# Delta-rule attention and two FFNs: rooms of their own for the fourth matrix's words, one inverse norm per unit of keys

## The chip, the cores and the metric

The kernel runs on one core of one Trainium2 chip. The metric is the device time of one launch in microseconds; the number to compare is the median of several runs. One further execution is profiled; its rows are what is read here. The engines are TensorE (PE, with its weight loads as PEld), VectorE (DVE), ScalarE (ACT), GpSimd (POOL) and SyncE (SP), whose queue issues every DMA of this kernel.

## The reference, cut to what matters

```python
def _attn_ref(q, k, v, beta):                 # (4, 8, 768, 48), float32
    k_n = k / (np.linalg.norm(k, axis=-1, keepdims=True) + 1e-06)
    state = zeros((B, H, D, D))
    for t in range(S):
        y[:, :, t] = q[:, :, t] @ state
        v_old = state^T @ k_n[:, :, t]
        state = state + beta_t * outer(k_n[:, :, t], v_t - v_old)
    return y

x = y.transpose(0, 2, 1, 3).reshape(B * S, H * D)          # 3072 tokens x 384
h = x @ moe_w_in;   x = maximum(0.01 * h, h) @ moe_w_out   # 384 -> 2048 -> 384
h = x @ moe2_w_in;  out = (h - tanh(h)) @ moe2_w_out
```

The four weight matrices arrive as float64; every key is divided by its norm.

## The kernel before, in words

The sequence is cut into steps of 64 positions and units of two steps: 6 units, 12 steps. In a step the delta rule becomes products of 64 x 64 blocks, with a triangular system of two 32 x 32 halves that `inverses` solves row by row, for a whole unit at once, mostly on GpSimd. Float32 accuracy comes from float16 pairs: each operand is split into a high and a low part, and a product is three float16 products.

Everything is one long program written out by Python generators. `Plan` estimates when each engine is free and each tile ready. `layer(n, i)` writes TensorE's FFN products for step n, layer i, in the order (0,0), (1,0), (0,1), (1,1), (2,0), and so on, and between them `Side.step` takes pieces of the attention and weight generators whose operands the plan holds ready: `keys`, `grams`, `inverses`, `merges`, `queries`, `products`, `states`, `outputs`, and `weights`. Keys named in `done` and waited for with `wait` order the generators among themselves. Each engine then runs its instructions in the order written. Generators take their place by a time and a delay, `d_...`, from the table START, or from STEADY once "w2" is in `done`. `weights` is also a filler: its VectorE operations may be put in front of a VectorE operation that the plan expects to wait.

`weights()` turns the four matrices from float64 into float16 pairs, in the order first layer in, first layer out, second in, second out. A matrix comes in 16 chunks of 128 x 768 int32 words, loaded by SP into "rooms": parts of weight tiles that are not in use yet. `w_f32` puts a chunk's words together as float32 in the destination tile (a `tensor_scalar` and two `scalar_tensor_tensor`); two chunks whose rooms lie side by side are taken as one, 768 wide, otherwise 384 wide each. ScalarE sums their squares into `wacc`, writing its by-product over the used room. When all are done, a norm across partitions gives the scale `sw`, and `splits` makes 16 pairs of parts: ScalarE twice (`wst<-wo`, `wo<-wst`), then VectorE or GpSimd once.

For the fourth matrix (`wo` number 1, second layer out) half of the chunks use rooms inside its own destination. The other eight use `Ub` and `Sb`, the operands with which `outputs` multiplies, so that the conversion waits for step 1's outputs and `outputs` from step 2 on waits for "w2". Layer (0,1) is the first that needs its splits.

`keys(n)` loads step n's keys, squares and sums them on ScalarE (16 pairs of instructions), computes 1 / (norm + 1e-6) in `key_scale` from a power of two as first guess and five Newton steps (22 VectorE operations on 128 x 16, tile `n`), and writes the scaled keys as float16 pairs (`kn`, `KN`). It starts once state n - 4 is done, as there are four `KN` tiles. The first two steps go through `first_keys`, both at once.

Of the kernel before, what the change touches and what calls it, by code (L numbers as in the profile page):

```python
# [7 lines left out]
F32 = mybir.dt.float32  # L8
F16 = mybir.dt.float16
BF16 = mybir.dt.bfloat16  # L10
I32 = mybir.dt.int32
ACTF = mybir.ActivationFunctionType
ALU = mybir.AluOpType
# [5 lines left out]
POW2 = 0x7F800000  # L19
# [172 lines left out]
def kernel(  # L192
# [12 lines left out]
    plan = Plan(tc.nc)  # L205
    pe, act, dve, pool, sp = (Engine(plan, n) for n in ("pe", "act", "dve", "pool", "sp"))
    NU, D = k.shape[0], k.shape[4]
    NM = k.shape[3]
# [32 lines left out]
    def tune(name):  # L241
        return (STEADY if "w2" in done else START)[name]
# [7 lines left out]
    def square_sum(o, i, junk):  # L250
        act.activation(out=junk if SIZE[junk.dtype] > 2 else junk.bitcast(BF16), in_=i, func=ACTF.Square, accum_out=o)
# [90 lines left out]
    def at(*aps):  # L342
        return plan.at(*aps)
# [6 lines left out]
    WO = [wts.tile([128, NF, 2, DM], F16, name=f"wo{i}") for i in range(2)]  # L350
    WI2 = [w.rearrange("p f c t n -> p f c (t n)") for w in WI]
    sw = const.tile([128, 6], F32, name="sw")

    def words(t):

        t = t.bitcast(I32)
        n = DM * 2
        return [t[:, i * n:(i + 1) * n] for i in range(t.shape[1] // n)]
# [64 lines left out]
    def weights():  # L423
        wi = [words(w.rearrange("p f c n -> p (f c n)")) for w in WI2]
        wo = [words(w.rearrange("p f c n -> p (f c n)")) for w in WO]
        nh = len(wi[0])

        x = [words(x_tile("w1"))[0] for _ in range(2)]
        a = Weights(0, w1_in, WI2[0], wo[0] + wo[1])
        b = Weights(1, w1_out, WO[0], ((wi[1] + x) * 2)[0:NF])  # L430
        yield Part([], 0)
        yield from a.convert()
        side.add(a.splits(), "s0")
        a = Weights(2, w2_in, WI2[1], (wo[1] * 2)[0:NF])
        yield from b.convert()
        side.add(b.splits(), "s1")
        done.add("w1")
        yield from a.convert()
        side.add(a.splits(), "s2")
        yield from wait(("y", 1))  # L440
        yield Part([], 0)
        bs = [words(t.rearrange("p c m n -> p (c m n)"))[0] for t in (Ub, Sb)]
        r = wo[1][nh // 2:] * 2 + bs * (NF // 4)
        b = Weights(3, w2_out, WO[1], r)
        yield from b.convert()
        for t in (Ub, Sb):
            pool.memset(t, 0.0)
        done.add("w2")
        side.add(b.splits(), "s3")

# [57 lines left out]
    def wait(key):  # L508
        if key not in done:
            yield lambda: key in done  # L510

    def load_k(n):
        if n < NS:
            kf_t[n] = ld_p.tile([128, NM, D], F32, tag="kf", name="kf", bufs=2)
            sp.dma_start(out=kf_t[n], in_=k[n // 2][:, n % 2])
# [35 lines left out]
    def key_scale(a, y, t):  # L551

        dve.tensor_scalar(out=t, in0=a, scalar1=2.0 ** -100, scalar2=None, op0=ALU.max)
        dve.tensor_scalar(out=y.bitcast(I32), in0=t.bitcast(I32), scalar1=1, scalar2=POW2,
                          op0=ALU.logical_shift_right, op1=ALU.bitwise_and)
        dve.tensor_scalar(out=t, in0=y, scalar1=2.0 ** 64 / 0.85, scalar2=None, op0=ALU.mult)
        dve.reciprocal(out=y, in_=t)
        for it in range(5):
            if it in (1, 3):
                yield plan.t["dve"]  # L560
            dve.tensor_tensor(out=t, in0=y, in1=y, op=ALU.mult)
            dve.scalar_tensor_tensor(out=t, in0=t, scalar=-0.5, in1=a, op0=ALU.mult, op1=ALU.mult)
            dve.scalar_tensor_tensor(out=y, in0=t, scalar=1.5, in1=y, op0=ALU.add, op1=ALU.mult)
        dve.tensor_tensor(out=t, in0=a, in1=y, op=ALU.mult)
        dve.tensor_scalar(out=t, in0=t, scalar1=1e-6, scalar2=1.0 / KS, op0=ALU.add, op1=ALU.mult)
        dve.reciprocal(out=y, in_=t)
# [8 lines left out]
            tt(kp[:, 1], kn, kp[:, 0], ALU.subtract, lead)  # L575
        done.add(("k", n))

    def keys(n):

        yield from wait(("s", n - 4))  # L580
        load_k(n)
        kf = kf_t.pop(n)
        n2 = sm_p.tile([128, 3, NM], F32, tag="n2", name="n2", bufs=1)
        a, y, t = (n2[:, i] for i in range(3))
        for m in range(NM):
            if m % tune("k_m") == 0:
                yield max(plan.t["act"], at(kf))
            junk = s_p.tile([128, D], BF16, tag="junk", name="junk", bufs=1)
            square_sum(a[:, m:m + 1], kf[:, m], junk)
        yield max(plan.t["dve"], at(a))  # L590
        yield from key_scale(a, y, t)
        yield max(plan.t["act"], at(y))
        key_split(n, kf, y, tune("lead_k"))

    def first_keys():

# [41 lines left out]
        split(AT[:, 0, av], AT[:, 1, av], ps[:, :, HB:], half[:, 0:1])  # L638

    def all_keys():  # L640
        for n in range(2, 2 * NU):
            yield from wait("w1")
            yield from keys(n)

    gd_t, nat_t = {}, {}

# [235 lines left out]
    def outputs(n):  # L882
# [3 lines left out]
        yield from wait(("x", u))  # L886
        Q, P = q_t.pop(n), p_t.pop(n)
        if n > 1:
            yield from wait("w2")
            yield from wait(("r", n - 3))  # L890
            yield from wait(x_owner[-NX])
            x_t[n] = x_tile(("a", n))
# [347 lines left out]
```

## Time and profile before

| | us |
|---|---|
| runs | 1243.42, 1246.35, 1244.53; median 1244.53 |
| profiled execution | 1241.99 |
| its span, first to last instruction | 1240.3 |
| TensorE busy in the span | 1012.0 |
| VectorE, ScalarE, GpSimd busy | 727.6, 635.0, 512.9 |
| mean granted TensorE clock | 0.959 |

Times in a row of the trace are microseconds from the start of the span. A row names the engine, the operation, what it writes and reads by the program's names, and how often. "idle before" is how long the engine did nothing ahead of it, and behind the arrow stands what ended that. All operations are recorded under line 160, where `Plan.issue` calls them, so rows are told apart by tiles. `h_ps` holds a first product of a layer, `o` a second, `a_ps` those of attention and norms.

### The profile page before, as it was taken

To read this page: it belongs to the slowest core of one execution; us is meant where nothing else is said; L and a number is where in the kernel's file an instruction comes from. 1 tells how busy PE (TensorE), PEld (TensorE's weight loads), DVE (VectorE), ACT (ScalarE), POOL (GpSimd) and SP (SyncE) were. 2 spreads that over 40 slices of the span, in tenths; PEclk is the share of its full clock that TensorE was granted. 3 is DMA by queue.
4 is the path that set the end of the run, shared out by engine and by line. 5 is a ranking of instruction groups with operands and counts; after the bars stand their busy time and mean duration, and the time that the engine had idled before them with its cause. 6 is when DMAs were issued, how large, how long until landed. Compare 5 with 4: busy or idle time off the path is not lost.

```text
span 1240.3 us, 36912 instructions
## 1 busy us (share of the span) xinstructions
PE 1012.0 (82%) x16216; PEld 832.3 (67%) x16216; DVE 727.6 (59%) x1609; ACT 635.0 (51%) x1414; POOL 512.9 (41%) x635
## 2 busy tenths in 40 slices
PE   0202679682876999989998899979999999999998
PEld 0202568571765788867687786768867888778875
DVE  7998844886768756776566577326654154420243
ACT  3556687746475555745455655325543354333342
POOL 4697365398238624771177304831210221012100
PEclk9999999895788999989999999989999999999999
DMA  9423010421000101000101000001000000000001
GB/s 359 160 72 112 3 28 18 164 60 39 16 25 23 45 16 46 23 23 3 27 15 37 12 24 10 14 14 32 25 10 14 14 11 2 1 17 11 1 1 26
DMA packets 21857, 48.17 MB, mean 39 GB/s; under 512 B 4288, under 2 KB 7360, under 8 KB 21696
## 3 DMA queue, kind: packets, MB, share of 16 engines
q1 hardware_dynamic: 21696, 45.82, 11.8%
q8 instruction: 126, 2.06, 0.7%
q14 instruction: 35, 0.29, 0.1%
HBM read 41.09 MB, written 4.72 MB: 37 GB/s over the span
## 4 chain that ended last, share of the span: by engine, by line
PE 54%; DVE 22%; ACT 13%; POOL 6%; issue 4%; DMA 1%; SPq 0%; ACTq 0%; POOLq 0%; DVEq 0%
PE o L160 22%; PE h_ps L160 21%; PE a_ps L160 10%; POOL X L160 2%; DVE n L160 2%; DVE wi L160 2%; DVE wo L160 2%; DVE x L160 2%; DVE sx L160 2%; ACT g L160 2%; POOL Gd L160 2%; ACT junk L160 2%; DVE g L160 2%; ACT sx L160 1%; DVE Ub L160 1%
## 5 line engine op out<-in xcount | busy, mean ns | idle before, releaser
L160 PE MATMUL h_ps<-x,wi 128*128 128x256 f16 x3456 | 422.5, 275 | 18.7 <-DVE x L160 6.3
L160 PEld LDWEIGHTS <-wi 128*128 128x128 f16 x3456 | 334.2, 98 | 76.5 <-issue 15.8
L160 PE MATMUL o<-wo,g 128*128 128x384 f16 x1152 | 213.2, 334 | 22.3 <-ACT wo L160 7.4
L160 POOL TENSOR_TENSOR g<-sx,g 128x512 f16<-128x512 f32 x80 | 96.2, 1203 | 314.5 <-ACT g L160 305.3
L160 PE MATMUL o<-g,wo 128*128 128x256 f16 x1728 | 211.0, 275 | 0.0
L160 PEld LDWEIGHTS <-wo 128*128 128x128 f16 x1728 | 167.2, 98 | 31.5 <-issue 9.3
L160 ACT ACTIVATE g<-sx 128x512 f16<-128x512 f32 x192 | 121.0, 630 | 119.5 <-DVE sx L160 116.5
L160 PEld LDWEIGHTS <-g 128*128 128x128 f16 x1152 | 112.5, 99 | 88.1 <-issue 27.1
L160 DVE SCALAR_TENSOR_TENSOR sx<-sx,kap,h_ps 128x512 f32<-128x512 f32 x96 | 71.2, 742 | 98.5 <-ACT sx L160 98.3
L160 POOL TENSOR_TENSOR X<-X,Gd 128x30 f32<-128x30 f32 (+9 forms) x180 | 116.1, 645 | 14.1
L160 POOL TENSOR_TENSOR Gd<-X 128x30 f32<-128x30 f32 (+9 forms) x180 | 108.4, 602 | 27.6 <-DVE X L160 15.2
L160 ACT ACTIVATE sx<-h_ps,kap 128x512 f32<-128x512 f32 x96 | 65.5, 683 | 92.2 <-PE h_ps L160 86.5
L160 ACT ACTIVATE sx<-h_ps 128x512 f32<-128x512 f32 x96 | 56.6, 590 | 105.5 <-PE h_ps L160 101.5
L160 DVE SCALAR_TENSOR_TENSOR g<-sx,g 128x512 f16<-128x512 f32 x96 | 71.4, 743 | 64.7 <-ACT g L160 64.6
L160 PEld LDWEIGHTS <-KTp 64*64 64x64 f16 x3360 | 66.4, 119 | 36.0 <-issue 34.5
L160 PE MATMUL a_ps<-ab,ones 128*128 128x1 bf16 x124 | 11.4, 168 | 95.7 <-DVE ab L160 93.7
L160 POOL TENSOR_TENSOR P<-P,maskp 128x1024 f16<-128x1024 f16 x24 | 54.7, 2288 | 67.9 <-DVE P L160 66.4
L160 PEld LDWEIGHTS <-KN 64*64 64x64 f16 x1824 | 39.1, 123 | 43.4 <-issue 39.1
L160 PEld LDWEIGHTS <-ones 128*128 128x128 bf16 x124 | 7.7, 103 | 79.9 <-DVE ab L160 51.5
L160 DVE COPY Ub<-R 64x768 f16<-64x768 f16 x47 | 23.4, 498 | 56.6 <-PE a_ps L160 56.1
L160 PE MATMUL a_ps<-Q,KTp 64*64 64x64 f16 x1152 | 24.6, 199 | 23.3 <-ACT Q L160 20.2
L160 PE MATMUL a_ps<-Q,Sb 128*128 128x64 f16 x528 | 36.7, 201 | 8.4 <-DVE Sb L160 8.4
(165 smaller groups left out, 1538.8 us busy)
## 6 DMA issues: line engine op xcount, KB each, us to landing
wo<-in_w_in_dram SPq DMA_DIRECT2D x32, 384.0 KB, 6.5
qf<-in_q_dram SPq DMA_DIRECT2D x24, 256.0 KB, 3.1
wi<-in_w_out_dram SPq DMA_DIRECT2D x14, 384.0 KB, 7.8
kf<-in_k_dram SPq DMA_DIRECT2D x12, 384.0 KB, 3.8
vf<-in_v_dram SPq DMA_DIRECT2D x12, 384.0 KB, 3.6
out_dram<-osb SPq DMA_DIRECT2D x48, 96.0 KB, 2.2
wo<-in_w_out_dram SPq DMA_DIRECT2D x8, 384.0 KB, 5.4
Ub<-in_w_out_dram SPq DMA_DIRECT2D x4, 384.0 KB, 3.3
```

The source lines that it names most:

```text
L160: return getattr(self.eng[eng], op)(*args, **kw)
```

## The change

The words of the last eight chunks of the fourth matrix get a tile `stage` of their own, 128 x 1536 float32. The conversion no longer waits for step 1's outputs, `outputs` no longer waits for "w2", and `Ub` and `Sb` are not cleared again. `keys` takes a unit: both steps' loads and squares, one `key_scale` on 128 x 32, then the two splits, each behind the wait for its state. `key_scale` takes its first guess from the bits of the number (halved by a shift and subtracted from a constant) and makes three Newton steps.

```diff
+    stage = wts.tile([128, 2 * DM * 2], F32, name="stage")
...
-        yield from wait(("y", 1))
-        yield Part([], 0)
-        bs = [words(t.rearrange("p c m n -> p (c m n)"))[0] for t in (Ub, Sb)]
-        r = wo[1][nh // 2:] * 2 + bs * (NF // 4)
+        r = (wo[1][nh // 2:] * 2)[0:NF // 2] + words(stage) * (NF // 4)
         b = Weights(3, w2_out, WO[1], r)
         yield from b.convert()
-        for t in (Ub, Sb):
-            pool.memset(t, 0.0)
         done.add("w2")
...
         dve.tensor_scalar(out=t, in0=a, scalar1=2.0 ** -100, scalar2=None, op0=ALU.max)
-        dve.tensor_scalar(out=y.bitcast(I32), in0=t.bitcast(I32), scalar1=1, scalar2=POW2,
-                          op0=ALU.logical_shift_right, op1=ALU.bitwise_and)
-        dve.tensor_scalar(out=t, in0=y, scalar1=2.0 ** 64 / 0.85, scalar2=None, op0=ALU.mult)
-        dve.reciprocal(out=y, in_=t)
-        for it in range(5):
-            if it in (1, 3):
+        dve.tensor_scalar(out=t.bitcast(I32), in0=t.bitcast(I32), scalar1=1, scalar2=None,
+                          op0=ALU.logical_shift_right)
+        dve.tensor_scalar(out=y.bitcast(I32), in0=t.bitcast(I32), scalar1=-1.0, scalar2=float(0x5F375A00),
+                          op0=ALU.mult, op1=ALU.add)
+        for it in range(3):
+            if it == 1:
                 yield plan.t["dve"]
...
-    def keys(n):
+    def keys(u):
 
-        yield from wait(("s", n - 4))
-        load_k(n)
-        kf = kf_t.pop(n)
-        n2 = sm_p.tile([128, 3, NM], F32, tag="n2", name="n2", bufs=1)
+        for s in range(2):
+            load_k(2 * u + s)
+        n2 = sm_p.tile([128, 3, MM], F32, tag="n2", name="n2", bufs=1)
         a, y, t = (n2[:, i] for i in range(3))
-        for m in range(NM):
-            if m % tune("k_m") == 0:
-                yield max(plan.t["act"], at(kf))
-            junk = s_p.tile([128, D], BF16, tag="junk", name="junk", bufs=1)
-            square_sum(a[:, m:m + 1], kf[:, m], junk)
+        kf = [kf_t.pop(2 * u + s) for s in range(2)]
+        for s in range(2):
+            for m in range(NM):
+                if m % tune("k_m") == 0:
+                    yield max(plan.t["act"], at(kf[s]))
+                junk = s_p.tile([128, D], BF16, tag="junk", name="junk", bufs=1)
+                square_sum(a[:, s * NM + m:s * NM + m + 1], kf[s][:, m], junk)
         yield max(plan.t["dve"], at(a))
         yield from key_scale(a, y, t)
-        yield max(plan.t["act"], at(y))
-        key_split(n, kf, y, tune("lead_k"))
+        for s in range(2):
+            yield from wait(("s", 2 * u + s - 4))
+            yield max(plan.t["act"], at(y))
+            key_split(2 * u + s, kf[s], y[:, s * NM:(s + 1) * NM], tune("lead_k"))
...
-        for n in range(2, 2 * NU):
+        for u in range(1, NU):
             yield from wait("w1")
-            yield from keys(n)
+            yield from keys(u)
...
         if n > 1:
-            yield from wait("w2")
             yield from wait(("r", n - 3))
```

## Rows read from the trace of the kernel before

**Rows 1.** The profile's page: busy us, TensorE's 40 slices, the chain by line.
```profile
PE 1012.0 (82%) x16216; PEld 832.3 (67%) x16216; DVE 727.6 (59%) x1609; ACT 635.0 (51%) x1414; POOL 512.9 (41%) x635
...
PE   0202679682876999989998899979999999999998
...
PE o L160 22%; PE h_ps L160 21%; PE a_ps L160 10%; POOL X L160 2%; DVE n L160 2%; DVE wi L160 2%; DVE wo L160 2%; DVE x L160 2%; DVE sx L160 2%; ACT g L160 2%; POOL Gd L160 2%; ACT junk L160 2%; DVE g L160 2%; ACT sx L160 1%; DVE Ub L160 1%
```

**Rows 2.** Stretches: length, busy us of each engine, PE clock, DMA share, GB/s.
```profile
165.00:224.70 59.70, 45.78 (x748) 40.09 (x744) 30.00 (x94) 47.25 (x118) 31.14 (x31) 0.94 0.12 37
224.70:275.20 50.50, 47.26 (x621) 40.29 (x622) 42.47 (x83) 31.05 (x87) 34.59 (x42) 0.97 0.34 106
275.20:301.60 26.40, 0.73 (x19) 0.61 (x17) 19.60 (x44) 11.86 (x42) 21.91 (x35) 0.58 0.15 45
301.60:420.00 118.40, 96.30 (x1946) 74.81 (x1946) 83.38 (x187) 69.21 (x165) 64.55 (x90) 0.85 0.09 26
420.00:1240.30 820.30, 778.03 (x11511) 635.79 (x11508) 414.27 (x958) 383.60 (x799) 257.66 (x314) 0.98 0.06 17
```

**Rows 3.** TensorE's timeline: start, length, operation, [idle before, releaser].
```profile
224.73 0.61 PE L160 MATMUL h_ps<-x,wi 128*128 128x256 f16 x2 [4.40 <-DVE ab L160]
...
273.08 2.12 PE L160 MATMUL h_ps<-x,wi 128*128 128x256 f16 x18 [0.74 <-DVE sx L160]
...
301.60 0.80 PE L160 MATMUL o<-wo,g 128*128 128x384 f16 x2 [2.02 <-ACT wo L160]
```

**Rows 4.** VectorE's timeline, the fourth matrix's last words.
```profile
293.90 0.87 DVE L160 SCALAR_TENSOR_TENSOR wo<-Sb,wo 128x384 int32<-128x384 int32 x1
```

**Rows 5.** One stretch, instructions on tile wo alone: PE, PEld, DVE, ACT, POOL.
```profile
219.00:301.60 82.60, 17.06 (x145) 14.02 (x144) 29.69 (x37) 9.81 (x26) 0.00 (x0) 0.82 0.31 98
```

**Rows 6.** Operations on tile wo: ns min/median/max, first and last start.
```profile
L160 DVE SCALAR_TENSOR_TENSOR wi<-wo,wi x32: 932/959/1555, 11.7 to 134.2; 128x768 int32<-128x768 int32 x32
L160 ACT ACTIVATE wst<-wo,sw x32: 597/600/623, 102.8 to 381.5; 128x384 f32<-128x384 f32 x32
L160 ACT ACTIVATE wo<-wst x32: 522/522/525, 103.5 to 382.2; 128x384 f16<-128x384 f32 x32
...
L160 DVE SCALAR_TENSOR_TENSOR wo<-wi,wo x14: 1123/1245/1449, 54.9 to 88.6; 128x768 int32<-128x768 int32 x14
...
L160 DVE SCALAR_TENSOR_TENSOR wo<-Ub,wo x8: 546/908/1504, 251.6 to 292.4; 128x384 int32<-128x384 int32 x8
```

**Rows 7.** TensorE's waits from 301.6 to 420 us: us, times, longest.
```profile
PE o L160 <- ACT wo L160: 7.4, 3, 2.8
...
PE o L160 <- DVE wo L160: 1.9, 1, 1.9
```

**Rows 8.** Groups of VectorE on tile n: busy us, mean ns, idle before.
```profile
L160 DVE SCALAR_TENSOR_TENSOR n<-n 128x16 f32<-128x16 f32 x100 | 26.6, 266 | 3.4
...
L160 DVE TENSOR_TENSOR n<-n 128x16 f32<-128x16 f32 x60 | 17.9, 299 | 1.4
...
L160 DVE TENSOR_SCALAR n<-n 128x16 f32<-128x16 f32 (+1 forms) x40 | 9.8, 245 | 1.1
...
L160 DVE RECIPROCAL n<-n 128x16 f32<-128x16 f32 x20 | 5.1, 253 | 0.7
```

**Rows 9.** The same groups in first_keys, 0 to 30 us.
```profile
L160 DVE SCALAR_TENSOR_TENSOR x<-x 128x32 f32<-128x32 f32 x10 | 1.9, 192 | 0.3
```

**Rows 10.** Timelines of ScalarE, VectorE, TensorE: step 3's squares, row solving, step 2.
```profile
203.44 0.24 ACT L160 ACTIVATE junk<-kf 128x48 bf16<-128x48 f32 x1
203.59 0.19 ACT L160 ACTIVATION_READ_ACCUMULATOR junk<-kf 128x1 f32 x1
...
248.09 2.10 DVE L160 STREAM_TRANSPOSE X<-Gd 128x1024 f32<-128x1024 f32 x1
...
375.32 0.92 ACT L160 ACTIVATE xhi<-x,sxs 128x768 f16<-128x768 f32 x1
...
420.04 1.15 PE L160 MATMUL h_ps<-x,wi 128*128 128x256 f16 x9
```

## The prediction

> **What bounds the kernel now.** The page comes first [rows 1]. TensorE is busy for 1012.0 us of 1240.3. Its slices show where the rest is: three of the first four hold 0 or 2 tenths, then the row fills up but for one slice with a 2, the tenth, around 280 to 310 us. The table of stretches sizes that [rows 2]. From 420 us on TensorE works 778.0 of 820.3 us: this part is TensorE's own, and an edit elsewhere buys little there. Before it two stretches stand out: 275.2 to 301.6 us, with 0.73 us of work in 26.40, and 301.6 to 420 us, with 96.30 in 118.40 at a mean granted clock of 0.85.
>
> The hole is read on TensorE's timeline [rows 3]. The last first-layer products before it start at 273.08; what ends it, at 301.60, is the first product with the fourth matrix, `o<-wo,g`, released by ScalarE's write of `wo`. VectorE's timeline says why so late: the last float64 words are put together at 293.90 [rows 4], and norm, scale and first split must follow. In the hole VectorE is busy for 19.60 of 26.40 us, and for 42.47 of the 50.50 before it [rows 2]. So the hole is the conversion of the fourth matrix, begun only after step 1's outputs, on a VectorE that is nearly full.
>
> **The fourth matrix.** The change drops the wait for ("y", 1), the empty `Part`, two memsets of `Ub` and `Sb`, and outputs(2)'s wait for "w2". It adds 6 KB per partition and no new arithmetic. The same words come by the same 16 loads on SP's queue and are converted by the same formula, but right behind the third matrix, whose last combining operation starts at 134.2 us [rows 6], instead of from 219 us on. The two rooms of `stage` lie side by side, so the last eight chunks go in four pairs of three 768-wide operations each, not in twenty-four 384-wide ones: 24 operations in place of 36.
>
> Cost: VectorE spent 29.69 us on `wo` in 37 operations from 219 to 301.6 [rows 5], one of them already a split; some 29 are the conversion. Two 384-wide operations cost at best 2 x 0.546 us where one of 768 costs 0.93 [rows 6], so twelve fewer save some 2 us: 27 us. With GpSimd quiet the lower end is 24 operations at 0.93, 22 us. Room: VectorE is idle for 29.7 us from 165 to 224.7, and 8.0 more to 275.2 [rows 2]. The planner offers these operations as fillers, and four loads run ahead. I take it that the words are done near 215 us, and the splits between there and 260. ScalarE's part is the sums, most of its 9.81 us in rows 5, and 16 splits of 0.60 + 0.52 us [rows 6], 18 us; it has 12.4 us idle to 224.7 and 19.4 to 275.2 [rows 2], and only the first two splits must be there when layer (0,1) asks. So the hole closes: **-25.7 us** (26.4 less the 0.7 of work that stays). What covers the moved work is those idle times; the third rival is their absence.
>
> A caution on that move. 32 combining operations of the third and first matrix have a median of 959 ns, the 14 of the second, beside GpSimd's row solving, 1245 [rows 6]. The Trainium skill's page "SBUF — State Buffer", section "🔬 SBUF: two separate sides", says that a VectorE operation with two SBUF inputs and a GpSimd operation that reads SBUF lock each other out for a whole instruction; the trace agrees in direction, by 0.29 us an operation. By the quiet row the 16 combining operations cost 15.3 us, by the crowded one 19.9; the idle time above holds either, and the sum stays.
>
> **What is late next.** Behind the hole TensorE waits 7.4 + 1.9 us more for splits of the fourth matrix [rows 7]; these go too: **-9.3 us**. The clock: a mean of 0.85 between the two levels (1.2 and 2.4 GHz) is 30% of 118.4 us at the lower one, 35.5 us, which costs half of that, 17.8, if TensorE was busy throughout, and nothing if it idled. In the hole the mean was 0.58 [rows 2], so part of the slow time behind it is its tail. I take half: **-9 us** (0 to -17.8). The other 12.8 us of idle there (22.1 less 9.3) wait on attention and evictions; I leave them.
>
> **The keys.** Each of ten steps issued 22 small VectorE operations: 26.6 + 17.9 + 9.8 + 5.1 = 59.4 us for 220 [rows 8]. Now each of five units issues 3 + 9 + 3 = 15, on 32 columns. first_keys shows a 32-column operation at 0.192 us [rows 9]: quiet, 75 of them are 14 us; at the mean of rows 8, 0.27 us, and a tenth more for the columns, 22. So 37 to 45 us of VectorE go, but TensorE is behind little of it. `DVE n` holds 2% of the chain of waits, 25 us [rows 1]; two thirds of the operations go, and much of that share lies in the hole, counted already. Outside I take **-5 us** (0 to -12); the 7 operations that first_keys loses, 1.3 us, are in it.
>
> The order moves too. ScalarE's squares stay as many, but all 32 of a unit now stand ahead of one key_scale. Step 2's keys come some 10 to 20 us later; step 3's, whose squares ended at 203.6 us, come earlier [rows 10]. Unit 1's row solving needs both and began at 248.1; it should begin 20 to 45 us sooner. That feeds layer (2,0): its input was split at 375.3, its first product ran at 420.0 [rows 10], so the supply had 45 us in hand. The 44 us gained ahead of it (25.7 + 9.3 + 9) just use that up: the sum holds even if unit 1 comes no sooner. Both `kf` loads of a unit are now issued together, the second behind the key_split of the unit before; q, v and `stage` loads behind it on SP's queue wait for that read, which I cost at nothing: the chunks wanted next are in their rooms by then.
>
> **The price in front.** 22 to 27 us of VectorE work and the sums, splits and squares of ScalarE move before and into layers (0,0) and (1,0). Queued behind them are Q, P and y of step 1, and layer (1,0) cannot start before x(1), now at 224.73 [rows 3]. The idle time says that nothing is lost; that fillers are placed by the planner's estimate, not by the clock, says that something is. Bounds: -3 (step 3's key operations no longer stand there) to +29.7 (nothing hidden). Nearest row: the 29.7 us of idle time, so near the lower end: **+7 us**.
>
> Sum: -25.7 - 9.3 - 9 - 5 + 7 = **-42 us**. The profiled execution took 1241.99 us (span 1240.3), which gives 1200; the median of the runs lies 2.5 us above it, at 1244.53, which gives **1202.5 us**.
>
> **Rivals.** First, more: unit 1 comes so early that all 22.1 us of idle and 17.8 of clock from 301.6 to 420 go, the keys' full 12 as well, and the price is nothing: 25.7 + 22.1 + 17.8 + 12 - 7 for what attention still takes = 71, so 1174. For it: VectorE loses 40 us. Against: GpSimd is busy for 64.55 of those 118.4 us and VectorE for 83.38 [rows 2], and most of that work stays.
>
> Second, less: the hole only breaks up. In `stage` a pair needs load, conversion and sum in turn before the next load, so the last splits trickle out of a ScalarE that is busy for 47.25 of 59.7 us [rows 2], and layer (0,1) waits in pieces. Half of the hole and half of the split waits: 12.9 + 4.7, so 1227. This is also how it would look if the conversion came little earlier after all.
>
> Third, slower: conversion and squares stand in front of Q and y of step 1. If none is hidden, layer (1,0) starts 29.7 us later, and 16 more squares at 0.24 + 0.19 us [rows 10], 6.9; hole and split waits give 35.0 back, but VectorE, as full as before behind it, leaves clock and keys unearned and splits late by the third of the hole: +1.6 + 9 = 11, so 1255. It decides once (1,0) starts over 35 us late. Against it: VectorE is half idle just there [rows 2].
>
> Fourth, nothing: gain and price cancel within 0.2%, 2.5 us, about what a measurement of this kernel can tell from no change: 1244.5.
>
> **Chances.** The forecast, 1188 to 1217: 0.56; more: 0.15; less: 0.19; slower: 0.06; nothing: 0.04. So faster 0.90, same 0.04, slower 0.06. The range takes in the bounds of clock and price and most of the first two rivals, and leaves out the third, the fourth, and the far ends: 1172 to 1237.
>
> **What would show it.** `o<-wo,g` first runs at 262 to 285 us, with no idle of TensorE over 5 us ahead of it. The last `wo` words come before 230. `n` operations: 75, under 23 us. Unit 1's row solving begins before 230. The clock from 275 to 400 is above 0.9. The step most likely to fail is the price: layer (1,0)'s first product within 10 us of 224.7. And if layer (2,0) starts before 385 but the end does not come earlier by as much, later stalls ate the gain, where I assumed none.

## The result and the profile after

The changed kernel took 1233.26 us (median of 4, 1232.07 to 1234.36) against 1243.97 for the kernel before on the same chip: ratio 0.9915, 95% interval 0.9891 to 0.9938, so 10.7 us less where 42 were forecast. Its profiled execution took 1233.33 us, span 1230.8. First the page, as in [rows 1].

```profile
PE 1005.9 (82%) x16216; PEld 824.4 (67%) x16216; DVE 699.2 (57%) x1440; ACT 632.8 (51%) x1399; POOL 521.4 (42%) x645
...
PE   0201648687978899888979989999999999999998
```

The 2 in the tenth slice has become a 7, and slices five to seven (123 to 215 us), which held 6, 7 and 9, now hold 6, 4 and 8. The stretches of [rows 2], cut at the same times, and two earlier ones:

```profile
140.00:160.00 20.00, 10.87 (x338) 10.20 (x333) 18.20 (x34) 12.93 (x32) 6.95 (x9) 0.59 0.23 71
160.00:180.00 20.00, 6.79 (x196) 6.00 (x196) 16.64 (x26) 16.74 (x44) 7.45 (x8) 0.50 0.34 110
...
165.00:224.70 59.70, 39.84 (x698) 33.62 (x697) 46.38 (x87) 47.21 (x109) 34.51 (x32) 0.84 0.21 69
224.70:275.20 50.50, 36.79 (x612) 31.00 (x607) 30.29 (x68) 40.27 (x116) 37.91 (x50) 0.86 0.07 20
275.20:301.60 26.40, 20.06 (x181) 17.38 (x178) 16.65 (x35) 15.78 (x40) 24.44 (x36) 0.98 0.00 1
301.60:420.00 118.40, 101.54 (x2053) 78.54 (x2052) 80.93 (x161) 64.98 (x168) 58.49 (x85) 0.93 0.09 26
420.00:1230.80 810.80, 767.75 (x11403) 626.78 (x11402) 387.62 (x870) 375.27 (x757) 260.44 (x318) 0.98 0.06 17
```

Against [rows 2], TensorE's busy time in the hole rises by 19.3 us and behind it by 5.2; in the two stretches in front it falls by 5.9 and 10.5, and ahead of 165 us by 4.0. From 160 to 180 us TensorE is busy for 6.79 of 20 us, where in the kernel before it was busy for 14.47. From 420 us on its idle time is as it was: 43.1 us, and 42.3 before. So the hole was filled, and most of what it gave was paid in front of it.

The granted clock rises from 0.85 to 0.93 behind the hole. In front the two traces cannot be compared by their clocks: from 35 to 130 us and from 130 to 185 the mean is 1.00 in the trace of before, and 0.53 and 0.54 in that of the changed kernel, long before any layer is late (columns as in [rows 2], before and then after):

```profile
35.00:130.00 95.00, 16.58 (x538) 15.26 (x536) 84.28 (x115) 51.63 (x127) 74.74 (x84) 1.00 0.31 102
```

```profile
35.00:130.00 95.00, 11.45 (x373) 10.46 (x374) 83.23 (x112) 49.89 (x124) 77.12 (x85) 0.53 0.32 106
```

Executions of one and the same kernel come with either: of 72 of the kernel before, 50 have a mean clock of 0.901 to 0.911 and take 1240.9 us in the mean, 22 have 0.950 to 0.962 and take 1241.1; the changed kernel's four have 0.910 to 0.915 or 0.970. So the 0.50 from 160 to 180 us, where before had 1.00, is no work of the change.

TensorE's timeline says where the time went (columns as in [rows 3]; first products of layers (0,0), (1,0), (1,1), (2,0), and the first product with the fourth matrix):

```profile
179.40 0.37 PE L160 MATMUL h_ps<-x,wi 128*128 128x256 f16 x1 [6.15 <-DVE x L160]
...
248.85 0.37 PE L160 MATMUL h_ps<-x,wi 128*128 128x256 f16 x1 [3.25 <-DVE x L160]
...
301.33 0.48 PE L160 MATMUL o<-wo,g 128*128 128x384 f16 x1 [4.85 <-ACT x L160]
...
359.14 0.37 PE L160 MATMUL h_ps<-x,wi 128*128 128x256 f16 x1 [3.47 <-DVE x L160]
...
399.55 0.27 PE L160 MATMUL h_ps<-x,wi 128*128 128x256 f16 x1
```

Layer (0,0) starts 8.3 us later than before (171.07), (1,0) 24.1 later [rows 3]. The first `o<-wo,g` stands where it stood, but it no longer waits for `wo`: ScalarE's copy of a layer's output to `x` releases it, and TensorE has worked until 4.85 us before. Layer (2,0) is 20.5 us earlier than in [rows 10], the end of the span only 9.5. VectorE's timeline shows what stands in front of x(0), the input of layer (0,0):

```profile
145.99 0.56 DVE L160 TENSOR_SCALAR wo<-wo 128x768 int32<-128x768 int32 x1
146.84 1.34 DVE L160 COPY Ub<-R 64x768 f16<-64x768 f16 x2 [0.30 <-PE a_ps L160]
148.21 2.55 DVE L160 SCALAR_TENSOR_TENSOR wo<-wo 128x768 int32<-128x768 int32 x2
150.79 1.07 DVE L160 TENSOR_SCALAR x<-a_ps,qs 32x128 f32<-32x128 f32 x3
151.89 0.56 DVE L160 TENSOR_SCALAR wo<-wo 128x768 int32<-128x768 int32 x1
152.37 1.14 DVE L160 SCALAR_TENSOR_TENSOR SP<-S,sc,SP 128x384 f16<-128x384 f32 x2
153.43 2.54 DVE L160 SCALAR_TENSOR_TENSOR wo<-wo 128x768 int32<-128x768 int32 x2
156.00 1.07 DVE L160 TENSOR_SCALAR x<-a_ps,qs 32x128 f32<-32x128 f32 x3
...
207.32 2.87 DVE L160 SCALAR_TENSOR_TENSOR wo<-stage,wo 128x768 int32<-128x768 int32 x1
```

The conversion is spread between the operations that make step 0's output and step 1's values, two combinations at a time, 2.5 us each pair. It ends at 210.2 us, as early as forecast, and took 28.4 us in 24 operations, just above the 22 to 27 forecast.

What stands in front of x(1), the input of layer (1,0), is another engine. The last part of step 1's output is written at 225.7 us (before: 214.96). The sum of its squares, `junk<-x`, starts 13.9 us later on ScalarE, and the high half of x(1), `xhi`, 6.4 us after that. Before, these two started at 218.92 and 221.20. VectorE's and ScalarE's timelines in the changed kernel, then ScalarE's in the kernel before:

```profile
225.37 0.35 DVE L160 TENSOR_SCALAR x<-a_ps,qs 32x128 f32<-32x128 f32 x1
```

```profile
239.63 0.83 ACT L160 ACTIVATE junk<-x 128x768 bf16<-128x768 f32 x1
...
246.03 0.92 ACT L160 ACTIVATE xhi<-x,sxs 128x768 f16<-128x768 f32 x1
```

```profile
213.26 1.70 ACT L160 ACTIVATE x<-a_ps,qs 96x384 f32<-96x384 f32 x4 [1.42 <-PE a_ps L160]
...
218.92 0.84 ACT L160 ACTIVATE junk<-x 128x768 bf16<-128x768 f32 x1
...
221.20 0.93 ACT L160 ACTIVATE xhi<-x,sxs 128x768 f16<-128x768 f32 x1 [0.52 <-DVE n L160]
```

In the changed kernel ScalarE makes in between squares of unit 1's keys, splits of the third and fourth matrix and evictions of attention, in the order written: it is busy for 24.3 of the 30 us from 220 to 250 (before: 18.9), while the conversion has been over since 210.2.

### The profile page after: what moved, and what is told of

It is laid out like the page before. It is cut to its first block, busy times and chain, and to the rows that moved or that the text cites. A ratio compares the mean times of both kernels' runs of the same rounds, so it can differ in the third digit from the quotient of the medians.

```text
span 1230.8 us, 36729 instructions
## 1 busy us (share of the span) xinstructions
PE 1005.9 (82%) x16216; PEld 824.4 (67%) x16216; DVE 699.2 (57%) x1440; ACT 632.8 (51%) x1399; POOL 521.4 (42%) x645
## 4 chain that ended last, share of the span: by engine, by line
PE 57%; DVE 24%; ACT 9%; POOL 4%; issue 4%; DMA 1%; ACTq 0%; SPq 0%; DVEq 0%; POOLq 0%
PE o L160 24%; PE h_ps L160 21%; PE a_ps L160 12%; DVE wo L160 4%; DVE wi L160 3%; DVE x L160 2%; DVE n L160 2%; ACT g L160 2%; POOL X L160 2%; DVE sx L160 2%; ACT junk L160 2%; DVE Ub L160 1%; DVE g L160 1%; ACT sx L160 1%; POOL Gd L160 1%
## 5 line engine op out<-in xcount | busy, mean ns | idle before, releaser
L160 PE MATMUL h_ps<-x,wi 128*128 128x256 f16 x3456 | 428.8, 277 | 26.0 <-DVE x L160 17.4
L160 PEld LDWEIGHTS <-wi 128*128 128x128 f16 x3456 | 337.6, 99 | 85.1 <-issue 29.8
L160 PE MATMUL o<-wo,g 128*128 128x384 f16 x1152 | 209.2, 331 | 17.1 <-ACT x L160 14.6
L160 POOL TENSOR_TENSOR g<-sx,g 128x512 f16<-128x512 f32 x79 | 92.7, 1173 | 307.0 <-ACT g L160 289.8
L160 PEld LDWEIGHTS <-g 128*128 128x128 f16 x1152 | 112.6, 99 | 84.6 <-issue 22.2
L160 PEld LDWEIGHTS <-KTp 64*64 64x64 f16 x3360 | 63.5, 116 | 32.7 <-issue 29.6
L160 DVE COPY Ub<-R 64x768 f16<-64x768 f16 x47 | 27.5, 584 | 85.0 <-PE a_ps L160 84.3
L160 POOL TENSOR_TENSOR Gd<-Gd,tri 128x256 f32<-128x256 f32 x24 | 17.8, 743 | 69.2 <-DVE Gd L160 69.0
L160 PE MATMUL a_ps<-Q,Sb 128*128 128x64 f16 x528 | 34.6, 197 | 12.2 <-DVE Sb L160 10.9
```

What stands on the lines that cost most here:

```text
L160: return getattr(self.eng[eng], op)(*args, **kw)
```

## The experiments

The planner writes the order of every engine from its own estimates, so an edit changes the work and the order at once. The first four runs take the change apart and leave the planner free, the next two hold the order fixed, and the rest move the order. "Before" is always the kernel before on the same chip. A layer has 144 of the 3456 first products, so the columns are the starts of the 1st, 145th, 433rd and 577th on TensorE's timeline.

| run | us | ratio to before, 95% | (0,0) | (1,0) | (1,1) | (2,0) |
|---|---|---|---|---|---|---|
| before | 1243.97 | 1 | 171.1 | 224.7 | 355.0 | 420.0 |
| changed | 1233.26 | 0.9915 (0.9891 to 0.9938) | 179.4 | 248.9 | 359.1 | 399.6 |
| e1 rooms alone | 1220.71 | 0.9842 (0.9822 to 0.9862) | 181.6 | 234.9 | 306.7 | 381.8 |
| e2 keys alone | 1247.61 | 1.0056 (1.0038 to 1.0074) | 169.9 | 229.8 | 386.9 | 469.4 |
| e3 guess alone | 1264.13 | 1.0191 (1.0165 to 1.0217) | 180.5 | 241.6 | 372.5 | 479.1 |
| e4 changed, waits for y 1 | 1256.84 | 1.0136 (1.0116 to 1.0156) | 169.8 | 229.8 | 394.7 | 473.6 |
| e5 guess, old order | 1232.26 | 0.9935 (0.9910 to 0.9960) | 169.4 | 222.8 | 349.9 | 414.4 |
| e6 rooms, old order | 1238.99 | 0.9980 (0.9965 to 0.9996) | 171.1 | 224.5 | 352.7 | 417.3 |
| e7 rooms and guess | 1234.86 | 0.9958 (0.9941 to 0.9974) | 184.9 | 242.3 | 315.7 | 390.8 |
| e8 rooms, joined keys | 1241.16 | 1.0005 (0.9990 to 1.0020) | 181.0 | 251.9 | 363.8 | 410.8 |
| e9 before, delay 0.16 | 1256.46 | 1.0122 (1.0108 to 1.0135) | 172.7 | 227.5 | 367.2 | 427.4 |
| e10 changed, longer gaps | 1218.71 | 0.9822 (0.9808 to 0.9835) | 157.2 | 219.9 | 319.2 | 400.7 |
| e11 changed, x first | 1237.04 | 0.9962 (0.9949 to 0.9975) | 169.6 | 241.0 | 315.2 | 390.6 |
| e12 guess in the order of e1 | 1208.74 | 0.9737 (0.9724 to 0.9751) | 178.6 | 231.7 | 302.4 | 376.8 |
| e13 before, delay 0.17 | 1237.24 | 0.9963 (0.9949 to 0.9977) | 173.4 | 229.9 | 334.7 | 412.4 |
| e14 changed, delay 0.16 | 1200.74 | 0.9663 (0.9646 to 0.9680) | 171.8 | 240.2 | 317.3 | 383.1 |
| e15 changed, delay 0.17 | 1223.29 | 0.9847 (0.9827 to 0.9867) | 176.8 | 239.9 | 357.4 | 401.5 |
| e16 before, delay 0.14 | 1251.63 | 1.0071 (1.0053 to 1.0089) | 174.1 | 233.7 | 364.9 | 428.4 |
| e17 changed, delay 0.14 | 1243.79 | 1.0008 (0.9991 to 1.0024) | 178.3 | 246.3 | 361.3 | 410.6 |
| e18 as e14, longer gaps | 1234.90 | 0.9951 (0.9933 to 0.9968) | 163.1 | 222.3 | 326.9 | 393.1 |

**The change taken apart (e1 to e4).** The first theory was that the conversion's new place makes (1,0) late, the rival that the keys do.

e1 is the kernel before with `stage`, without both waits and both memsets:

```diff
-        yield from wait(("y", 1))
-        yield Part([], 0)
-        r = wo[1][nh // 2:] * 2 + bs * (NF // 4)
+        r = (wo[1][nh // 2:] * 2)[0:NF // 2] + words(stage) * (NF // 4)
```

> The kernel before with only the rooms of its own for the fourth matrix (stage, no wait for step 1's outputs, outputs without the wait for w2); keys as before. Conversion theory (the moved conversion stands in front of step 1's Q, P and y on VectorE and ScalarE): layer (1,0) starts 12 to 25 us later than 224.7, the first product with the fourth matrix runs near 295 to 303, and the time is 1232 to 1246. Keys theory (the squares of both steps and the earlier keys and grams of unit 1 stand in front): layer (1,0) starts within 8 us of 224.7, the first such product near 265 to 280, and the time is 1200 to 1222.

e2 is the kernel before with the new `key_scale`, `keys(u)` and `all_keys` of the change, and nothing of the rooms.

> The kernel before with only the keys' part (one inverse norm per unit, new first guess, three steps); the fourth matrix waits for step 1's outputs and uses Ub and Sb as before. Conversion theory: layer (1,0) starts within 8 us of 224.7, the hole before the first product with the fourth matrix stays at 15 to 26 us, the time is 1228 to 1242. Keys theory: layer (1,0) starts 12 us or more late, the hole comes on top, the time is 1250 to 1275.

e3 has the new `key_scale` alone, still one step at a time.

> The kernel before with only the new key_scale (new first guess, three steps in place of five), still one step of keys at a time: 150 small VectorE operations in place of 220. Both theories: nothing moves in front, so the time falls by what these operations held up, 2 to 10 us, 1234 to 1242; the hole shrinks by at most 4 us, as two sets of them lie in and before it.

e4 is the changed kernel, own rooms kept, with two waits back:

```diff
+        yield from wait(("y", 1))
+        yield Part([], 0)
...
+            yield from wait("w2")
```

> The changed kernel, but the fourth matrix's conversion again waits for step 1's outputs; it keeps its own rooms, and outputs do not wait for w2. Conversion theory: layer (1,0) starts at 222 to 234 again, and a hole of 10 to 25 us comes back before the first product with the fourth matrix; the time is 1222 to 1240. Keys theory: layer (1,0) stays at 243 or later and the hole comes on top, 1245 to 1265.

Own rooms alone are faster than the whole change, 18.6 us less than before; (1,0) is 10.2 us late, not 24.1. The keys alone put it 5.1 us late, and the two together more than both. e4 brings (1,0) back to 5.1 us, yet the time gets worse by some 25 us: its first `o<-wo,g` runs at 341.5 us. So the conversion does make layers late in front, and being early is still worth more: with own rooms alone the first `o<-wo,g` runs at 285.2 us. Neither theory names the whole loss, and both fail on e3, which takes work away and costs 25 us. Its stretch behind the hole:

```profile
301.60:420.00 118.40, 72.88 (x1838) 56.64 (x1839) 81.32 (x171) 69.71 (x169) 62.57 (x90) 0.75 0.08 22
```

TensorE's busy time there is 23.4 us below [rows 2] (15.5 below from 224.7 us on, since more of the work falls into the hole), though VectorE has less to do in the kernel.

**The same edits in a fixed order (e5, e6).** The planner goes on booking what it booked before, and only the issue differs. In e5 it books the removed operations without issuing them; in e6 it books `stage` as if it were `Ub` and `Sb` (two tiles, so that the operations stay 384 wide), and books the two memsets that are gone.

```diff
+        plan.book("reciprocal", out=y, in_=t)
+        for it in range(5):
...
+            if it > 2:
+                plan.book("tensor_tensor", out=t, in0=y, in1=y)
+                plan.book("scalar_tensor_tensor", out=t, in0=t, in1=a)
+                plan.book("scalar_tensor_tensor", out=y, in0=t, in1=y)
+                continue
```

> The kernel before with the new first guess alone, with every instruction of the five engines in the order of the kernel before; the only difference is that 55 small VectorE operations are gone (the planner still books them, and does not issue them). The same edit with the planner free to reorder gave 1264 us against 1239. Theory A, the 25 us came from the order that the planner wrote after the edit, not from the operations: here 1232 to 1240, between 55 x 0.18 = 10 us less and no change. Rival B, the new operations themselves cost the time (a longer one, or a later result): here about 1264 again, above 1250.

> The kernel before with rooms of their own for the last eight chunks of the fourth matrix, with every instruction in the order of the kernel before (the planner books the new rooms as if they were Ub and Sb): what is gone is SyncE's wait for the readers of Ub and Sb, and two memsets on GpSimd. Own rooms with the planner free gave 1220.7 against 1239.4. Theory A, the gain of own rooms is the order that they allow, not the wait on the room: VectorE waited only 2.6 us for the words in 215 to 302, so here 1234 to 1240. Rival B, the wait for the rooms is what holds the end: here near 1221, and the first o<-wo,g clearly before 300.

In e5 the removed operations are 77, not 55: seven for each of ten steps and for `first_keys`; the page counts 1532 VectorE instructions in place of 1609. The guess gives 8.1 us in the old order, and costs 25 in the order that the planner writes for it. The operations are not what was slow in e3. In e6 own rooms give 2.5 us where the free planner made 18.6 of them. TensorE's timeline of e6, then the last combinations of its fourth matrix (columns as in [rows 6]):

```profile
301.32 0.48 PE L165 MATMUL o<-wo,g 128*128 128x384 f16 x1 [2.02 <-ACT wo L165]
```

```profile
L165 DVE SCALAR_TENSOR_TENSOR wo<-stage,wo x16: 546/850/1507, 251.5 to 293.6; 128x384 int32<-128x384 int32 x16
```

Against 301.60 and 293.90 [rows 3, 4] nothing moved: the room itself was never the limit, the place of the conversion in the order was.

**Which part of the keys costs (e7, e8).** e7 is e1 with the new `key_scale`; e8 is the changed kernel with the old one.

> Own rooms and the new guess, keys still one step at a time, planner free. Splits the 12 us that the keys' part costs on top of own rooms (1220.7 without it, 1233.3 with it) into the guess and the joining. Theory A, any edit of the keys makes the planner write another order, and the price is that order's: no sign is forecast, 1205 to 1245, and the end goes with the first products of layers (1,0) and (1,1) (234.9 and 306.7 with own rooms alone, 248.9 and 359.1 in the changed kernel). Rival B, joining both steps is what costs, by the attention's work of unit 1 that it pulls ahead: here 1212 to 1221, and layer (1,1) near 307.

> The changed kernel with the old first guess: own rooms, keys of both steps at once. Rival B of the run before this (joining is what costs): 1233 to 1240, layer (1,1) near 359. Theory A (the order of each plan): no sign, 1205 to 1245. If this and the run before it are both near 1221, only the two together cost, and neither edit can be named alone.

On top of e1, the guess costs some 14 us, the joining some 20, and both together only 9 to 13. They do not add up, and (1,1) at 315.7 us does not go with the time. No single edit of the keys carries the loss.

**The order alone (e9).** One booked delay of the planner, in the kernel before:

```diff
-    GAP = 0.15
+    GAP = 0.16
```

> The kernel before with one number of the planner changed, the delay that it books between an instruction and the next that needs it (0.15 to 0.16 us). No arithmetic, room or operation is added or taken away (a few operations go to another engine); only the written-out order differs. It measures what another order alone is worth. Theory A (the order that the planner happens to write sets the size of the effects seen): off the kernel before by 5 us or more, 1220 to 1260, either sign. Rival B (an order changes the time only when the work or the waits change): 1237 to 1246.

The same arithmetic, with a few operations on another engine, 15 us slower. Two stretches of it:

```profile
275.20:301.60 26.40, 7.54 (x61) 5.91 (x58) 22.53 (x34) 15.38 (x57) 23.88 (x34) 0.69 0.22 74
301.60:420.00 118.40, 87.79 (x1906) 67.45 (x1903) 86.34 (x198) 64.71 (x147) 65.62 (x91) 0.83 0.09 26
```

Against [rows 2] TensorE's busy time gains 6.8 us in the hole and loses 8.5 behind it, and from 420 us on it idles for 47.4 us instead of 42.3: here another order loses its time behind the hole. From here on the theory is that each order is a draw of its own.

**Two moves inside the changed kernel (e10, e11).**

```diff
-                    if max(e[1], plan.t["dve"]) + 0.45 > until:
+                    if max(e[1], plan.t["dve"]) + 1.3 > until:
```

> The changed kernel, with conversion operations put only into VectorE gaps of 1.3 us or more by the planner's times, where 0.45 us was enough (its 128x768 combinations are booked at 0.865 us and took 0.95 to 2.9 us). Theory A, the lateness in front comes from the conversion standing among the operations of x(0) and x(1) on VectorE: layer (0,0) back from 179.4 to 170 to 175 and (1,0) from 248.9 to 225 to 238, with the conversion's end later than 210, and a time of 1215 to 1230. Rival B, the keys' order makes (1,0) late, wherever the conversion stands: (0,0) moves, (1,0) stays at 245 or more, and the time at 1230 to 1240.

```diff
-START = {... 'd_xa': 0, 'd_xb': 1, ...
+START = {... 'd_xa': -3, 'd_xb': -3, ...
-STEADY = {... 'd_xa': -1, 'd_xb': 1, ...
+STEADY = {... 'd_xa': -3, 'd_xb': -3, ...
```

> The changed kernel, with the two chains that make a layer's input (its sum of squares and its two halves) ranked ahead of the attention's steps by the planner (delay -3 in place of 0, -1 and 1). Theory A, attention work of units 1 and 2 ranked ahead of these chains is what holds layer (1,1) until 359.1: (1,1) before 335, and 1212 to 1228. Rival B, the chains are late because what they need is late (y1, a bank): (1,1) after 345, and 1228 to 1245.

e10 moves the conversion of all four matrices. (0,0) comes 22.2 us earlier and (1,0) 29.0, more than its theory named, and the time falls by 12 to 15 us (by the ratios, by the medians) to 1218.7. But (2,0) comes 1.1 us later than in the changed kernel: the gain stands behind it, where TensorE has 144 attention products less to do (6.7 us of its time) and idles for 8.2 us less. VectorE's words of the fourth matrix in e10, then TensorE's first products of (0,0) and (1,0):

```profile
L160 DVE SCALAR_TENSOR_TENSOR wo<-stage,wo x8: 940/1101/2874, 212.1 to 267.3; 128x768 int32<-128x768 int32 x8
```

```profile
157.18 0.37 PE L160 MATMUL h_ps<-x,wi 128*128 128x256 f16 x1 [7.48 <-DVE x L160]
...
219.90 0.37 PE L160 MATMUL h_ps<-x,wi 128*128 128x256 f16 x1 [1.57 <-DVE x L160]
```

e11 brings (1,1) 44.0 us earlier, as its theory said, and (2,0) 9.0, and still ends 4 to 6 us later than the changed kernel, outside the 1212 to 1228 of its theory. From 420 us on TensorE is idle for 51.0 us, 8 more than in the changed kernel:

```profile
420.00:1235.70 815.70, 764.68 (x11325) 624.62 (x11323) 402.49 (x890) 375.91 (x768) 262.39 (x328) 0.97 0.06 16
```

An early layer is no gain by itself: the attention steps that were passed over come due later. When (2,0) starts, 6474 attention products are still to come in e11, 6329 in the changed kernel and 6183 before.

**The guess in the order of e1 (e12).** Built as e5, on e1.

> Own rooms with the new guess, every instruction in the order of own rooms alone (55 small VectorE operations gone, nothing else). In the order of the kernel before, the same removal gave 8 us. If that holds for any order: 1208 to 1218 (1220.7 less 3 to 12), the fastest version so far, against 1234.9 for the same two edits in the order that the planner writes for them. If the gain hangs on the order: 1218 to 1224.

In e12 the 77 operations give 12 to 13 us here (0.9842 to 0.9737) and 8 in the old order. The free planner turned the same two edits into 1234.86 (e7): 26 us between two orders of the same work.

**Several orders of both kernels (e13 to e17), and e10 again (e18).** The edit is the one number of e9, 0.14, 0.16 or 0.17, in either kernel; e18 is e14 with the edit of e10.

> The kernel before with the planner's booked delay at 0.17 us (0.15 to 0.16 gave 1256.5 against 1241.3). With the next three runs it asks whether the 10.7 us of the change belong to its work, or to the order that it happened to get. Theory A, each order is a draw of its own: the before kernels at 0.15, 0.16 and 0.17 lie 10 us or more apart, 1225 to 1260. Rival B, 0.15 is a tuned value, and others are worse by about as much: 1250 to 1260.

> The changed kernel with the planner's booked delay at 0.16 us, no other edit (1233.3 at 0.15). If the change's own work is worth about 10 us in any order, the mean of the changed kernel over 0.14, 0.16 and 0.17 lies some 10 us below that of before. Theory A, a draw: 1205 to 1250.

> The changed kernel with the planner's booked delay at 0.17 us. Theory A, a draw: 1205 to 1250, 5 us or more away from the run at 0.16.

> The kernel before with the planner's booked delay at 0.14 us. Theory A, a draw: 1225 to 1260. Rival B (0.15 is a tuned value): 1245 to 1260.

> The changed kernel with the planner's booked delay at 0.14 us. With it the changed kernel is seen at the same four values as before (1251.6, 1241.4, 1256.5 and 1237.2 at 0.14 to 0.17, mean 1246.7). So far 1233.3, 1200.7 and 1223.3, mean 1219.1. If the change's work is worth 20 to 35 us over orders: 1200 to 1245 here, and below the 1251.6 of before at this value; a draw above 1251 would leave the means 20 us apart with no order-free gain at this value.

> The fastest version so far (the changed kernel at 0.16 us, 1200.7) with conversion operations put only into VectorE gaps of 1.3 us or more, as in the run at 0.15 us, where this gave 14.6 us. Theory A, the conversion ahead of x(0) and x(1) costs time in any order: 1185 to 1200. Rival B, the longer gaps helped there by drawing another order: 1200 to 1230.

At 0.14, 0.15, 0.16 and 0.17 the kernel before lies at 1.0071, 1, 1.0122 and 0.9963 of its own time, the changed one at 1.0008, 0.9915, 0.9663 and 0.9847. The means are 1.0039 and 0.9858: 1.8% apart, 22 us. The standard deviations are 0.0071 and 0.0146, so that the standard error of the difference is the square root of (0.0071² + 0.0146²), over 2, which is 0.0081 or 10 us: the change's gain over orders is some 22 us, give or take 20 (two standard errors). It is below before at each of the four values, by 8 to 57 us. But 57 us of that is one value, 0.16; the other three give 8, 11 and 14. And with four orders of each kernel a 95% interval is wider than two standard errors, some 27 us, and takes in zero. So a gain over orders is likely, and its size is not shown. That 0.15 was a tuned value of before is not borne out, since 0.17 is faster; nor is each step of the constant worth 10 us, since 0.15 and 0.17 lie 5 apart. In e14, at 1200.7 below the range expected of it and the fastest run of all, the stretches are:

```profile
165.00:224.70 59.70, 44.77 (x796) 37.26 (x796) 44.76 (x98) 42.93 (x99) 36.11 (x32) 1.00 0.19 64
224.70:275.20 50.50, 38.01 (x502) 32.79 (x501) 28.25 (x65) 41.98 (x124) 41.46 (x53) 0.90 0.06 20
275.20:301.60 26.40, 20.52 (x152) 15.45 (x151) 19.48 (x36) 15.16 (x34) 21.42 (x33) 0.87 0.06 16
301.60:420.00 118.40, 105.05 (x2223) 84.83 (x2222) 79.42 (x180) 66.71 (x174) 53.12 (x80) 0.96 0.10 28
420.00:1197.20 777.20, 744.61 (x11171) 609.40 (x11168) 391.12 (x849) 366.60 (x748) 256.50 (x312) 0.99 0.06 17
```

Its (0,0) starts 7.6 us earlier than in the changed kernel and its (1,0) 8.6 (the clock of 1.00 in front, against 0.84, is that of the other kind of execution named in the section on the result). It keeps the filled hole, and idles for 32.6 us from 420 us on, where the changed kernel idles for 43.1. e18 falsifies the general form of e10's theory: with longer gaps (1,0) starts 17.9 us earlier than in e14, and the time is 34 us longer, above even the rival's range. Whether longer gaps help hangs on the order that comes with them.

## Why the prediction failed, step by step

By the marks on TensorE, the 9.5 us of span come together as +24.1 (layer (1,0) late) - 44.6 (won from there to layer (2,0)) + 11.0 (lost behind it). The forecast had +7, -44 and -5. So two terms failed, the price in front by 17 us and what lies behind layer (2,0) by 16; together they are the 32.5 us between -42 and -9.5.

**The hole, -25.7: right in the main.** TensorE works 20.06 of its 26.4 us, 19.3 more than before, the last words start at 207.32, before 230 as named, and no wait over 5 us stands ahead of `o<-wo,g`. That this product itself would come at 262 to 285 was wrong, because layer (0,1) starts 20.4 us late.

**Splits and clock behind the hole, -9.3 and -9: right in kind, nearly in size.** The waits for splits [rows 7] are gone. New ones took part of their place: from 301.6 to 420 us TensorE's longest waits are now

```profile
PE o L160 <- ACT x L160: 4.8, 1, 4.8
PE h_ps L160 <- DVE x L160: 3.5, 1, 3.5
```

Its idle time from 301.6 to 420 us fell by 5.2 us, not 9.3. Taken in stretches of 1 us, TensorE was busy at the lower level for 32.1 us there before and for 12.2 now, 20 us less, worth 10. With the hole that makes 34.5 of the 44. That the marks give 44.6 is partly luck: a layer's mark also comes early when attention work is passed over, and of that more below.

**The price in front, +7: the first step that failed, mis-sized by 17 us.** The prediction named it as the likeliest to fail. "The idle time says that nothing is lost" summed VectorE's idle time from 165 to 224.7 us, 29.7 us, and took the row of idle time as the nearest. But 15 of the 24 operations ran between 146 and 170 us, ahead of that idle time, among the operations of x(0) and of step 1's values, with VectorE already busy for 17.1 of the 20 us from 140 to 160 in the kernel before. Idle time hides moved work only if the work is put there. That the conversion's place does this is shown by e1 (own rooms alone: (0,0) 10.5 us late) and e4 (waits back: 1.2 early). It explains the 8.3 us of (0,0) and, with step 1's output 10.8 us late, less than half of the 24.1.

The other 13.3 us come after the conversion, on ScalarE. From the last part of step 1's output to the first product of (1,0) it took 9.8 us before and 23.1 now, behind squares of keys and splits in ScalarE's order. The prediction said that this work moves in front, but sized the price by VectorE's idle time alone. In e1 and e7, without joined keys, the same stretch takes 10.6 and 13.1 us, in e8, with them, 24.1; e2, joined keys without own rooms, has 12.0, and e11, the changed kernel with x ranked first, 13.1. So the rank of x(1) among ScalarE's work decides this part, as e11 shows; that the joining alone puts it there is not shown, as no run held the order and joined the keys.

The clock adds little to this price. TensorE was busy at the lower level for 6 us more from 165 to 275.2 us than before (12.5 against 6.5, in stretches of 1 us), worth 3 at most, and most of that is the early low stretch, which costs nothing that the runs can see: e2 and e4 have the same instructions in the same order on every engine up to 260 us, at a mean clock of 1.00 and of 0.53 from 35 to 130 us, and their layers (0,0) and (1,0) start within 0.03 us of each other.

The second and third rival each held half of what came: the time is near the second's 1227, the mechanism in front is the third's, conversion and squares, at 24 us of lateness, under the 35 from which it decides. Of the cost, its lower end of 22 us counted all 24 operations at 0.93 us; eight of them, `TENSOR_SCALAR`, take 0.55 when quiet, so that it should have been 19.

**Behind layer (2,0), -5: the second step that failed, +11.0.** The keys' 5 us were the only term there, and later stalls were put at nothing. When (2,0) starts, 20.5 us early, TensorE has 146 attention products more to do than before (6.9 us of its time), and from there to the end it idles for 4.1 us more. By the first product of layer (3,1) the lead has become 16.2 us of lateness, and from there it settles at a lead of 9.5. The layers had run ahead of the attention.

The keys' work itself came in kind and not in size. The 75 operations came, but took 29.8 us, not 14 to 22; the row "at the mean of rows 8 and a tenth more" was a bound that their crowding passed (last section). VectorE saves 29.6 us on them. On the end the keys' part costs 9 to 13 us on top of e1. In a fixed order the guess is worth 8 to 13 us (e5, e12), about the bound of the forecast; what turned the guess round is the order.

**Unit 1.** Its row solving begins at 239.63, 8.5 us sooner and not 20 to 45, and layer (2,0) at 399.55, not before 385. Its input was split at 372.08, so that the claim that supply is not what holds (2,0) stood: it is TensorE's own lateness.

**What the sum left out.** All its terms are sums over one order, with the rest of the order as it was. The order did not stay: 8 us of gain became 25 of loss (e5, e3), 2.5 of gain became 18.6 (e6, e1). For before, four orders of equal arithmetic lie 20 us apart, for the changed kernel 43 us. Over these orders the change gives some 22 us with an interval that takes in zero, and 8 to 14 at three of the four values: the 10.7 measured is one draw, and the 42 is not borne out. What stays open is which single decisions of the planner make an order good: an early (1,0) or (1,1) does not by itself (e4, e11, e18), and no run pinned the joined keys to a fixed order.

## What to carry to other kernels

Where a planner writes the order, test an edit twice: with the order held fixed, by booking what was there before, which gives the work's own worth, and over a few values of a planner constant that changes no arithmetic, which gives the scatter of orders; a gain below that scatter is no verdict on the edit, and the best order can be kept (here 1200.7 us, and 1208.7 by holding the order of e1). When work is moved, count only the idle time behind the point where it is written, and look at what stands on every engine, not only the fullest, between there and the next layer's input. An early layer mark is a gain only if no other work was passed over for it. Before clocks of two traces are compared, see whether executions of one kernel already differ in them.

## What the runs showed of the hardware

Small VectorE operations stretch to the length of GpSimd's. In the changed kernel's `key_scale`, a 128x32 operation that takes 0.19 us when quiet takes over 1 us if a GpSimd operation has just begun, and ends with it. VectorE's timeline, then GpSimd's:

```profile
190.27 1.14 DVE L160 TENSOR_TENSOR n<-n 128x32 f32<-128x32 f32 x1
...
192.55 0.19 DVE L160 TENSOR_TENSOR n<-n 128x32 f32<-128x32 f32 x1
...
194.07 1.12 DVE L160 TENSOR_SCALAR n<-n 128x32 f32<-128x32 f32 x1
```

```profile
190.11 1.25 POOL L160 TENSOR_TENSOR g<-sx,g 128x512 f16<-128x512 f32 x1 [0.18 <-ACT g L160]
...
194.00 1.15 POOL L160 TENSOR_TENSOR g<-sx,g 128x512 f16<-128x512 f32 x1 [0.24 <-ACT g L160]
```

The first ends at 191.41 us, GpSimd's at 191.36; the last at 195.19, GpSimd's at 195.15; the one between has no such neighbour. The combination of 2.87 us at 207.32 (0.89 at its quickest) lies over a GpSimd operation of 2.36 us that began at 207.01. That is the lock for a whole instruction that the Trainium skill states in "SBUF — State Buffer", section "🔬 SBUF: two separate sides"; the trace agrees, and shows that its price goes by the length of GpSimd's operation and not by that of VectorE's: for 75 small operations 29.8 us where quiet ones would take some 15. The `TENSOR_SCALAR`, with one input, was held like the others. The excess is some 0.2 us an operation here and was 0.09 in the kernel before (59.4 us for 220, some 40 when quiet), so the mean of rows 8 did not carry over to another order.
